# Attention and a gated MLP: the first batch's product with v, split into two 64-column halves of the array

## The chip, the cores and the metric

The kernel runs on one core of a Trainium2 chip. The metric is the device time of one execution in microseconds. Three timed runs of the kernel before gave 475.4, 476.24 and 478.64 us; the median is 476.24 us. One more execution was taken with the hardware profiler, and all rows below are from it. The engines are named as in the profile: PE is TensorE's matmul, PEld its weight load, DVE is VectorE, ACT is ScalarE, POOL is GpSimd, SP is SyncE, which issues the transfers.

## The reference

Attention with a local window of 96 positions and 8 global positions, for 4 batches of 8 heads, 768 positions, 64 numbers per head; behind it a gated MLP that mixes positions.

```python
scores = scale * np.matmul(q, k.transpose(0, 1, 3, 2))
keep = is_global | is_local
scores = np.where(keep, scores + bias, -1000000000.0)
a = np.exp(scores - np.max(scores, axis=-1, keepdims=True))
a = a / (np.sum(a, axis=-1, keepdims=True) + 1e-09)
x = np.matmul(a, v)                    # heads side by side: (4, 768, 512)
h = np.maximum(x @ w_in, 0.0)          # (.., 1024)
u, v = h[..., :512], h[..., 512:]
v_n = (v - mu) / np.sqrt(var + 1e-06)
v_s = np.einsum('ts,bsd->btd', w_spatial, v_n) + b_spatial[None, :, None]
out = (u * v_s) @ w_out
```

## The kernel before

A batch has 6 blocks of 128 positions; a block has 4 pairs of heads. Block n is one of 24. For a block, `prep(n)` loads q and k, `prep_v(n)` loads v, `scores(n)` forms scores and probabilities, and `values(n)` multiplies them with v. Only two 128-wide chunks of keys matter to a block: its own and the one before it, into whose first rows the global positions are copied. The first block of a batch has one chunk. Behind the attention stand the MLP's parts: `mlp_v` (the half that is normalised), `mlp_u` (the other half), `mlp_s` (the mixing of positions) and `mlp_o` (the last product). Their weights are loaded and split into a high and a low half by `setup_w_in`, `setup_w_t` and `setup_w_out` while the first batch's attention runs.

The first batch (`whole(n)`, n under 6) works in full float32; the later batches work with numbers split in two halves of type float32r. In the first batch, for each pair g of heads, `values(n)` does this. The probabilities of both heads are transposed into a PSUM tile `p` (PE), which ACT copies to the SBUF tile `pth`, one of two buffers. Then PE multiplies: the stationary operand is 128 columns of `vring` (64 of each head), the moving operand is all 256 columns of `pth` (128 positions for the first head, 128 for the second), and the result goes to `ops`, 128 partitions by 256 columns. Of this result only half is used: partitions 0 to 63 (first head's v) with columns 0 to 127 (first head's positions), and partitions 64 to 127 with columns 128 to 255. For every second g the sums of the softmax, transposed as well (`raw` to `p`, copied to a tile that is shown as `c`), divide the used parts of two pairs: one DVE instruction for partitions 0 to 63 and one for 64 to 127, each 64 partitions by 256 numbers. The quotient is split into `xth` and `xtl`, the MLP's input.

A float32 matmul stands in the trace as two MATMUL records with a LDWEIGHTS record each; a float32r matmul and a transpose as one.

The order of the work is not that of the code. Every operation is recorded, given a rank from the table `KEYS` (one number for each block and part), and `plan` lays them out on each engine by rank and by its own cost figures. PE and all other engines then carry out their queues in that fixed order. Where the plan has a wait of over 900 ns on PE in the first 150 us, `keep_warm` puts dummy transposes of `ident` there, whose results nobody reads; they run whether or not the wait comes.

All recorded operations have one line in the profile, L39, that of the recorder's `issue`. So tiles are told apart by name: `s` are scores in PSUM, `pr` probabilities, `p` transposes, `pth` their copies, `ops` the product with v, `c` the quotient (and the divisor), `m` all PSUM tiles of the MLP, `raw`, `rawh` and `u` the staging of weights.

Of the kernel before, what the change touches and what calls it, by code (L numbers as in the profile page):

```python
# [10 lines left out]
F32 = mybir.dt.float32  # L11
# [19 lines left out]
class Op:  # L31
# [6 lines left out]
    def issue(self):  # L38
        getattr(self.real, self.call)(*self.args, **self.kw)  # L39

# [17 lines left out]
class Recorder:  # L58
# [26 lines left out]

    def add(self, engine, call, args, kw):
        op = Op()
        op.ways = ((engine, call, args, kw),)
        op.token = self.now
        op.take(0)  # L90
        outs = [kw[x] for x in ("out", "accum_out") if x in kw]
        ins = [x for n, x in kw.items() if n not in ("out", "accum_out") and isinstance(x, bass.AP)]
        aps = [x for x in args if isinstance(x, bass.AP)]
        if "out" not in kw:
            outs.insert(0, aps.pop(0))
        op.writes, op.reads = outs, ins + aps
        op.num = len(self.ops)
        self.ops.append(op)
# [72 lines left out]
def elements(ap):  # L171
    n = 1
    for x in list(ap.ap)[1:]:
        n *= x[1]
    return n
# [19 lines left out]
def cost(op):  # L195

    out = op.writes[0]
    n = elements(out)
    src = op.reads[0] if op.reads else out
    psum = any(in_psum(x) for x in op.reads + op.writes[:1])  # L200
    parts = list(out.ap)[0][1]
    if op.eng == "tensor":
        if op.call == "transpose":
            return 109, 0, False
        n = elements(op.kw["rhs"])
        if op.kw["rhs"].dtype == F32:
            return 4 * max(n, 128) * .422, 0, False
        return {128: 110, 256: 119, 384: 175, 512: 231}[n], 0, False
    if op.eng == "sync":
        return 650, 2050 + n * 4 * parts * .0042, False  # L210
    if op.eng == "scalar":
        if "accum_out" in op.kw:
            return 280 + .83 * n, 90, False
        if in_psum(src):
            return (175 + .85 * n, 0, False) if parts < P else (70 + .86 * n, 0, False)
        return 112 + .83 * n, 0, False
    if op.eng == "gpsimd":
        if n <= 8:
            t = 600 if op.kw.get("op") == ALU.pow else 280
        elif op.call == "tensor_tensor":  # L220
            t = 148 + 2.21 * n
        elif op.kw.get("op0") == ALU.max:
            t = 210 + 3.34 * n
        elif isinstance(op.kw.get("scalar1"), bass.AP):
            t = 270 + .9 * n
        else:
            t = 155 + .84 * n
        return t, 0, True
    one = "accum_out" in op.kw or psum or op.call in ("bn_stats", "bn_aggr", "reciprocal", "tensor_reduce", "memset")
    if op.call == "reciprocal":  # L230
        return 90 + 6.25 * n, 85, False
    pointers = sum(isinstance(op.kw.get(x), bass.AP) for x in ("scalar1", "scalar2"))
    if op.call in ("tensor_scalar", "tensor_copy") and not one:
        return (70 + n if pointers == 2 else 70 + 58 * pointers + .53 * n), 0, True
    if op.call in ("tensor_reduce", "bn_stats"):
        return 120 + 1.06 * elements(src), 0, False
    if op.call == "bn_aggr":
        return 145, 0, False
    return (180 if parts < P else 66) + (1.04 if parts < P else 1.1) * n, 0, not one


def link(ops):

    wrote, used, bank = {}, {}, {}
    for op in ops:
        preds = set()
        for ap in op.reads:
            name, p0, p1, bits = extent(ap)
            for q0, q1, b, o in wrote.get(name, ()):
                if q0 < p1 and p0 < q1 and b & bits:  # L250
                    preds.add(o)
        op.after = set(preds)
        for ap in op.writes:
            name, p0, p1, bits = extent(ap)
            for table in (wrote, used):
                for q0, q1, b, o in table.get(name, ()):
                    if q0 < p1 and p0 < q1 and b & bits:
                        preds.add(o)
        for ap in op.reads:
            name, p0, p1, bits = extent(ap)  # L260
            used.setdefault(name, []).append((p0, p1, bits, op.num))
        for ap in op.writes:
            name, p0, p1, bits = extent(ap)
            for table in (wrote, used):
                if name in table:
                    table[name] = [x for x in table[name] if not (p0 <= x[0] and x[1] <= p1 and x[2] | bits == bits)]
            wrote.setdefault(name, []).append((p0, p1, bits, op.num))
        if op.eng == "tensor":
            name = extent(op.writes[0])
            half = name[0], name[3].bit_length() > 1024  # L270
            if half in bank:
                preds.add(bank[half])
            bank[half] = op.num
        preds.discard(op.num)
        op.preds = preds
# [874 lines left out]
```

## Time and profile before

| | |
|---|---|
| median of three timed runs | 476.24 us |
| the profiled execution's own span | 473.8 us |
| PE busy | 460.7 us (97%) |
| DVE, ACT, POOL busy | 73%, 59%, 54% |
| granted TensorE clock, mean | 0.998 |
| share of PE in the chain that ended last | 87% |
| instructions | 9730 |

The page cuts the span in 40 slices of 11.8 us and gives each engine a digit for its busy tenths. PE's ends are modelled: a stream of matmuls overlaps, so a record is longer than its pace. The pace of a run of n like matmuls is worked out as (length of the run minus one record) divided by (n minus 1). The first batch's attention fills the first 86 us or so of the span, together with the preparation of the weights and the first parts of the MLP.

### The profile page before, as it was taken

Reading aid. Unit: us, or ns where it says so; the run is one execution under the profiler, and the core shown is the slowest. Engines: PE = TensorE matmul, PEld = TensorE weight load, DVE = VectorE, ACT = ScalarE, POOL = GpSimd, SP = SyncE. Lnnn points to the kernel's source line nnn. Section 1 sums busy time; section 2 is a strip of 40 time slices with the busy share of each in tenths; the row PEclk is TensorE's granted clock in tenths of the full one; section 3 lists DMA queues with packets and bytes.
Section 4 is the critical chain, followed back from the end, with each engine's and each line's share of the span. In section 5 each row is a group of like instructions: output and inputs, shape, how many; then the busy total and the mean of one; then the engine's idle time right before and its main releaser. Section 6 shows DMA issues by size and latency. Waiting matters only on the chain.

```text
span 473.8 us, 9730 instructions
## 1 busy us (share of the span) xinstructions
PE 460.7 (97%) x3181; PEld 424.3 (90%) x3181; DVE 344.6 (73%) x1016; ACT 279.9 (59%) x775; POOL 254.1 (54%) x378
## 2 busy tenths in 40 slices
PE   7889999999999999999999999999999999999995
PEld 6668888999999889999999999999989899999994
DVE  6899998948679987986766668784376998843332
ACT  5859896455477776786446448872155888721111
POOL 4334743377575788788545357883037775650000
PEclk9999999999999999999999999999999999999999
DMA  6947323747758687746582167630077683000111
GB/s 212 318 155 229 116 65 114 193 108 183 184 148 226 166 226 193 172 129 166 150 219 101 49 184 187 177 98 19 22 183 209 176 213 78 13 1 1 46 46 50
DMA packets 35915, 65.48 MB, mean 138 GB/s; under 512 B 6064, under 2 KB 6320, under 8 KB 35856
## 3 DMA queue, kind: packets, MB, share of 16 engines
q1 hardware_dynamic: 35856, 64.77, 49.7%
q8 instruction: 27, 0.44, 0.4%
q14 instruction: 32, 0.26, 0.2%
HBM read 29.76 MB, written 6.68 MB: 77 GB/s over the span
## 4 chain that ended last, share of the span: by engine, by line
PE 87%; DVE 4%; SPq 3%; DMA 2%; ACT 2%; issue 1%; DVEq 0%
PE m L39 61%; PE ops L39 9%; PE s L39 9%; PE p L39 8%; SPq L39 3%; DMA vring<-in_v_dram 2%; DVE c L39 1%; ACT pr L39 1%; DVE raw L39 1%; DVE ev L39 0%; DMA kring<-rawh 0%; DVE pr L39 0%; DVE w_in_h L39 0%; DVE rawh L39 0%; DVE xtl L39 0%
## 5 line engine op out<-in xcount | busy, mean ns | idle before, releaser
L39 ACT ACTIVATE pr<-pr,mn 128x256 f32<-128x256 f32 (+1 forms) x192 | 92.0, 483 | 17.5 <-DVE mn L39 17.1
L39 DVE TENSOR_TENSOR c<-ops,c 64x256 f32<-64x256 f32 x168 | 70.6, 421 | 11.0 <-ACT c L39 4.7
L39 DVE CUSTOM_DVE_ANT_0 pr<-s,bias 128x256 f32<-128x256 f32 (+1 forms) x192 | 68.6, 394 | 11.0 <-PE s L39 8.4
L39 POOL TENSOR_SCALAR pr<-pr,rc 128x256 f32<-128x256 f32 (+1 forms) x144 | 68.1, 493 | 10.4 <-DVE rc L39 8.3
L39 PE MATMUL s<-kring,q 128*128 128x256 f32 (+1 forms) x384 | 69.8, 307 | 1.3 <-DVE mn L39 1.0
L39 PE MATMUL ops<-pth,vring 128*128 128x256 f32 x352 | 67.0, 311 | 0.7 <-DVE pth L39 0.5
L39 PEld LDWEIGHTS s<-kring,q 128*128 128x128 f32 x384 | 57.6, 191 | 7.1 <-DVE mn L39 2.4
L39 ACT ACTIVATE pth<-p 128x512 fp32r<-128x512 f32 (+3 forms) x96 | 52.3, 559 | 15.1 <-PE p L39 11.5
L39 PEld LDWEIGHTS ops<-pth,vring 128*128 128x128 f32 x352 | 53.1, 189 | 5.4 <-DVE pth L39 1.2
L39 PE MATMUL p<-ident,pr 128*128 128x128 f32 x352 | 56.6, 273 | 0.7 <-ACT c L39 0.7
L39 DVE TENSOR_TENSOR pth<-p,pth 128x512 fp32r<-128x512 f32 (+1 forms) x72 | 45.1, 642 | 7.0 <-ACT pth L39 6.0
L39 DVE TENSOR_TENSOR ev<-m,b_bc 128x512 f32<-128x512 f32 x24 | 16.6, 691 | 46.1 <-PE m L39 46.0
L39 PEld LDWEIGHTS p<-ident,pr 128*128 128x128 f32 x352 | 42.2, 140 | 5.2 <-ACT c L39 1.3
L39 ACT ACTIVATE ev<-m 128x512 f32<-128x512 f32 (+1 forms) x36 | 21.3, 591 | 42.8 <-PE m L39 40.8
L39 PE MATMUL m<-w_t_h,vnh 128*128 128x256 f32 x288 | 43.9, 282 | 0.0
L39 PE MATMUL m<-w_t_h,vnl 128*128 128x256 f32 x288 | 43.7, 282 | 0.0
L39 PE MATMUL m<-w_t_l,vnh 128*128 128x256 f32 x288 | 43.7, 283 | 0.0
L39 POOL TENSOR_TENSOR xtl<-c,xth 128x256 fp32r<-128x256 f32 x40 | 29.8, 747 | 25.2 <-ACT xth L39 25.1
L39 ACT ACTIVATE gh<-ev 128x512 fp32r<-128x512 f32 x24 | 15.1, 630 | 42.6 <-DVE ev L39 42.6
L39 PEld LDWEIGHTS m<-w_t_h,vnh 128*128 128x128 f32 x288 | 38.9, 189 | 0.7
L39 ACT ACTIVATE c<-ops 64x256 f32<-64x256 f32 x72 | 27.3, 380 | 20.4 <-PE ops L39 17.9
L39 POOL TENSOR_TENSOR vnl<-ev,vnh 128x512 fp32r<-128x512 f32 x24 | 31.1, 1296 | 14.7 <-ACT vnh L39 9.4
(138 smaller groups left out, 997.8 us busy)
## 6 DMA issues: line engine op xcount, KB each, us to landing
q<-rawh SPq DMA_DIRECT2D x72, 128.0 KB, 2.4
q<-raw SPq DMA_DIRECT2D x72, 128.0 KB, 2.4
out_dram<-ev SPq DMA_DIRECT2D x23, 256.0 KB, 2.8
raw<-in_q_dram SPq DMA_DIRECT2D x18, 256.0 KB, 2.9
raw<-in_v_dram SPq DMA_DIRECT2D x18, 256.0 KB, 3.0
raw<-in_k_dram SPq DMA_DIRECT2D x18, 256.0 KB, 3.3
kring<-rawh SPq DMA_DIRECT2D x36, 128.0 KB, 2.4
kring<-raw SPq DMA_DIRECT2D x36, 128.0 KB, 2.4
```

The lines of the kernel that those rows point to most:

```text
L39: getattr(self.real, self.call)(*self.args, **self.kw)
```

## The change

Three things are changed, all else is new text that is switched off (`ROWS = False`: a like change for the scores).

First, the product with v in the first batch. For two pairs of heads at once, when both `pth` are ready, one group of matmuls is issued without anything in between (`together`). Each head has a matmul of its own: 64 columns of `vring` are stationary, the 128 columns of its own positions are moving, and the result goes to partitions 64j to 64j+63 and columns 0 to 127 of `ops`. So there are twice as many matmuls, each with half the stationary columns and half the moving columns, and heads alternate. A group has 8 matmuls (16 MATMUL records); in the first block, which has one chunk, 4 matmuls (8 records). There are 12 groups, two in each of the six blocks.

Second, the division: the used parts now lie in the same columns, so one DVE instruction of 128 partitions by 256 numbers takes the place of two of 64 by 256.

Third, `KEYS` has new numbers in every place, and `plan` charges a group `SWITCH` more than its matmuls. So the order on every engine is a new one.

```diff
 class Op:
     def issue(self):
+        if self.call == "together":
+            for call, args, kw in self.args:
+                getattr(self.real, call)(*args, **kw)
+            return
         getattr(self.real, self.call)(*self.args, **self.kw)
...
+    def together(self, engine, calls):
+
+        self.add(engine, "together", calls, {})
...
 def cost(op):
...
+        if op.call == "together":
+            return SWITCH + sum(2 * elements(kw["rhs"]) * .422 for _, _, kw in op.args), 0, False
...
+SWITCH = 130
+ROWS, COLS = False, True
-KEYS = {'start': -18.36, ('P', 0): -14.95, ('bias', 0): 12.66, ('S', 0, 0): -4.23, ('S', 0, 1): 10.8, ...
+KEYS = {'start': -301.68, ('P', 0): -119.08, ('bias', 0): -61.19, ('S', 0, 0): 120.07, ('S', 0, 1): 67.02, ...
...
 values(n), first batch
                 if g % 2 == 0:
                     ops = opsring[g // 2]
-                for c in range(nch):
+                    pair = []
+                pair.append(pth)
+                if COLS and g % 2:
+                    nc.together(nc.tensor, [
+                        ("matmul", (ops[64 * j:64 * j + 64, x, 0:P],), dict(
+                            lhsT=vring[:, order[c], (g - 1 + x) * P + 64 * j:(g - 1 + x) * P + 64 * j + 64],
+                            rhs=pair[x][:, c, j * P:(j + 1) * P], start=(c == 0), stop=(c == nch - 1),
+                        ))
+                        for x in range(2) for c in range(nch) for j in range(2)
+                    ])
+                for c in range(0 if COLS else nch):
                     nc.tensor.matmul(
                         ops[:, g % 2], lhsT=vring[:, order[c], g * P:(g + 1) * P], rhs=pth[:, c],
...
+                    if COLS and folded(n):
+                        nc.vector.tensor_tensor(out=xs, in0=ops[:, :, 0:P], in1=div, op=ALU.mult)
                     for half, s_ in enumerate(halves):
-                        src = ops[s_, :, half * P:half * P + P]
+                        if COLS and folded(n):
+                            continue
+                        src = ops[s_, :, 0 if COLS else half * P:P if COLS else half * P + P]
```

What it makes of the queues is shown at three places. In these rows a repeat count stands at the end, a float32 matmul counts once, and L39 of before is L41 (a group) or L43 (all else) in the changed kernel.

PE, the third block's product with v and what lies around it, before and then after; `p` are transposes, `s` the next blocks' scores, `ops` the product:

```order
L39 MATMUL ops_93<-pth_125,vring_114 128x256 x2
L39 MATMUL ops_93<-pth_127,vring_114 128x256 x2
L39 MATMUL p_124<-ident,pr_107 128x128 x2
L39 MATMUL p_124<-ident,pr_108 128x128 x2
L39 MATMUL ops_94<-pth_125,vring_114 128x256 x2
L39 MATMUL p_126<-ident,raw_113 128x128 x2
L39 MATMUL p_124<-ident,pr_109 128x128 x2
L39 MATMUL p_124<-ident,pr_110 128x128 x2
L39 MATMUL ops_94<-pth_127,vring_114 128x256 x2
```

```order
L41 MATMUL ops_93<-pth_125,vring_114 64x128 x4
L41 MATMUL ops_93<-pth_127,vring_114 64x128 x4
L43 MATMUL s_106<-kring_97,q_0_96 128x256 x2
L43 MATMUL p_124<-ident,pr_107 128x128 x2
L43 MATMUL p_124<-ident,pr_108 128x128 x2
L43 MATMUL p_126<-ident,raw_113 128x128 x2
L43 MATMUL p_124<-ident,pr_109 128x128 x2
L43 MATMUL p_124<-ident,pr_110 128x128 x2
L41 MATMUL ops_94<-pth_125,vring_114 64x128 x4
L41 MATMUL ops_94<-pth_127,vring_114 64x128 x4
```

The second half of the block's product was in two parts with transposes between them, each behind its own `pth`; now all of it stands behind both.

PE, the first block: what lies between its scores and the second block's, before and then after; `m<-ident` are dummies:

```order
L39 MATMUL m_135<-ident 128x128 x8
L39 MATMUL p_124<-ident,raw_113 128x128 x2
L39 MATMUL p_126<-ident,pr_109 128x128
L39 MATMUL p_126<-ident,pr_110 128x128
L39 MATMUL p_124<-ident,pr_111 128x128
L39 MATMUL p_124<-ident,pr_112 128x128
L39 MATMUL ops_93<-pth_125,vring_114 128x256
L39 MATMUL ops_93<-pth_127,vring_114 128x256
```

```order
L41 MATMUL ops_93<-pth_125,vring_114 64x128 x2
L41 MATMUL ops_93<-pth_127,vring_114 64x128 x2
L43 MATMUL m_135<-ident 128x128 x13
L43 MATMUL p_126<-ident,raw_113 128x128 x2
L43 MATMUL p_124<-ident,raw_113 128x128 x2
L43 MATMUL p_126<-ident,pr_104 128x128 x2
L43 MATMUL p_126<-ident,pr_105 128x128
```

The dummies moved behind the first group and grew from 8 to 13. Over the whole program, after the 17 at the start, there were dummies of 8, 5, 5 and 6; now there are 6, 13, 5, 7 and 7, the last 7 ahead of the sixth block's `mlp_v`.

DVE, the end of the first piece of `w_in` that the MLP needs (`CAST w_in_h`), before and then after; `ISA pr` are the scores with bias and their minimum, `c<-ops` the division, `SCALAR_TENSOR_TENSOR raw` the last steps of unpacking the weight:

```order
L39 TENSOR_TENSOR c_0_128<-ops_94,c_2_134 64x256
L39 TENSOR_SCALAR raw_0_116<-raw_0_116 128x512
L39 TENSOR_TENSOR c_0_128<-ops_94,c_2_134 64x256
L39 SCALAR_TENSOR_TENSOR raw_0_116<-u_115,raw_0_116 128x512
L39 ISA pr_104,mn_101<-s_103,bias 128x256
L39 ISA mn_101 128x1
L39 SCALAR_TENSOR_TENSOR raw_0_116<-u_115,raw_0_116 128x512
L39 TENSOR_TENSOR xtl_123<-c_0_128,xth_122 128x2x128
L39 CAST w_in_h<-raw_0_116 128x512
```

```order
L43 TENSOR_TENSOR xtl_123<-c_1_129,xth_122 128x2x128
L43 SCALAR_TENSOR_TENSOR raw_0_116<-u_115,raw_0_116 128x512
L43 ISA pr_111,mn_101<-s_103,bias 128x256
L43 ISA mn_101 128x1
L43 SCALAR_TENSOR_TENSOR raw_0_116<-u_115,raw_0_116 128x512
L43 TENSOR_TENSOR c_0_128<-ops_94,c_2_134 128x256
L43 CAST w_in_h<-raw_0_116 128x512
```

Ahead of this cast DVE has, of all rows of its queue that differ, two `ISA pr` with their two reads of the minimum, two net divisions, one `CAST xth` and one `xtl` less, and one copy to `c` and one copy to `raw` more. The matmul that waits for this cast is the MLP's first in both orders. On SP the first piece of `w_in` (512 KB) is now issued ahead of the second block's q and k instead of right behind them; transfers in all are the same in number and size.

## Rows read from the trace of the kernel before

**Rows 1.** The page: span, PE, granted clock, and the last chain by engine.

```profile
span 473.8 us, 9730 instructions
PE 460.7 (97%) x3181; PEld 424.3 (90%) x3181; DVE 344.6 (73%) x1016; ACT 279.9 (59%) x775; POOL 254.1 (54%) x378
PEclk9999999999999999999999999999999999999999
PE 87%; DVE 4%; SPq 3%; DMA 2%; ACT 2%; issue 1%; DVEq 0%
```

**Rows 2.** Stretches: length, each engine's busy us (instructions), clock, DMA share, GB/s.

```profile
core 0: us, PE busy (x) PEld busy (x) DVE busy (x) ACT busy (x) POOL busy (x), PEclk, DMA share, GB/s
10.00:20.00 10.00, 8.70 (x44) 6.57 (x43) 8.58 (x36) 9.21 (x35) 4.07 (x4) 1.00 1.04 347
20.00:30.00 10.00, 8.17 (x48) 6.59 (x47) 9.84 (x23) 5.10 (x14) 2.68 (x2) 1.00 0.80 236
...
50.00:60.00 10.00, 10.00 (x58) 8.77 (x57) 9.04 (x28) 8.41 (x21) 6.88 (x8) 1.00 0.36 119
60.00:70.00 10.00, 10.00 (x64) 8.70 (x63) 9.88 (x36) 9.04 (x27) 3.77 (x6) 1.00 0.11 35
```

**Rows 3.** PE in order of time: start, length, instructions [idle before, releaser].

```profile
15.22 1.04 PE L39 MATMUL m<-ident 128*128 128x128 f32 x8
...
17.64 1.13 PE L39 MATMUL ops<-pth,vring 128*128 128x256 f32 x4
...
20.34 1.03 PE L39 MATMUL ops<-pth,vring 128*128 128x256 f32 x4
...
28.56 0.50 PE L39 MATMUL m<-w_in_h,xth 128*128 128x512 f32 x1 [1.83 <-DVE w_in_h L39]
...
39.49 1.89 PE L39 MATMUL ops<-pth,vring 128*128 128x256 f32 x8
```

**Rows 4.** The product with v alone, in two stretches of the first batch.

```profile
0.00:36.00 36.00, 6.37 (x24) 4.16 (x24) 3.35 (x8) 0.00 (x0) 1.00 0.72 229
36.00:86.00 50.00, 16.22 (x64) 11.43 (x64) 5.88 (x14) 0.00 (x0) 1.00 0.42 132
```

**Rows 5.** PE and PEld: later one-pass (float32r) matmuls, 256 and 128 moving columns.

```profile
460.60 0.87 PE L39 MATMUL m<-w_t_h,vnh 128*128 128x256 f32 x6
...
103.81 1.00 PE L39 MATMUL s<-kring,q 128*128 128x128 f32 x8
...
103.69 0.98 PEld L39 LDWEIGHTS s<-kring,q 128*128 128x128 f32 x8
```

**Rows 6.** Groups by form: count, busy us, mean ns of one record, idle before.

```profile
L39 PE MATMUL ops<-pth,vring 128*128 128x256 f32 x64 | 16.2, 383 | 0.0
...
L39 PE MATMUL m<-w_t_h,vnh 128*128 128x256 f32 x6 | 0.9, 281 | 0.0
...
L39 PEld LDWEIGHTS s<-kring,q 128*128 128x128 f32 x8 | 1.0, 191 | 0.0
```

**Rows 7.** DVE in order of time, around the first divisions and the cast.

```profile
20.59 0.24 DVE L39 CAST xth<-c 128x256 fp32r<-128x256 f32 x1
...
21.21 0.42 DVE L39 TENSOR_TENSOR xtl<-c,xth 128x256 fp32r<-128x256 f32 x1
21.55 0.42 DVE L39 CUSTOM_DVE_ANT_0 pr<-s,bias 128x256 f32<-128x256 f32 x1
...
21.89 0.42 DVE L39 COPY raw<-rc 128x512 f32<-128x512 f32 x1
...
22.56 0.41 DVE L39 TENSOR_TENSOR c<-ops,c 64x256 f32<-64x256 f32 x1
22.90 0.41 DVE L39 TENSOR_SCALAR raw<-raw 128x512 int32<-128x512 int32 x1
...
26.48 2.02 DVE L39 CAST w_in_h<-raw 128x512 fp32r<-128x512 f32 x1
```

**Rows 8.** The last chain in its last stretch: start, length, what.

```profile
439.93 25.06 PE m L39 x182
```

More of the change, by code (lines that the diff above doesn't have):

```diff
@@ L38, in issue, with sides @@
     def issue(self):
+        if self.call == "together":
+            for call, args, kw in self.args:
+                getattr(self.real, call)(*args, **kw)
+            return
         getattr(self.real, self.call)(*self.args, **self.kw)
+def sides(call, args, kw):
+    outs = [kw[x] for x in ("out", "accum_out") if x in kw]
+    ins = [x for n, x in kw.items() if n not in ("out", "accum_out") and isinstance(x, bass.AP)]
+    aps = [x for x in args if isinstance(x, bass.AP)]
+    if "out" not in kw:
+        outs.insert(0, aps.pop(0))
+    return outs, ins + aps
 class Engine:
@@ L90, in add @@
         op.take(0)
[L91 to L96, printed above, removed]
+        op.writes, op.reads = [], []
+        for one in args if call == "together" else ((call, args, kw),):
+            outs, ins = sides(*one)
+            op.writes += outs
+            op.reads += ins
         op.num = len(self.ops)
@@ L268, in link @@
         if op.eng == "tensor":
[L269 to L273, printed above, removed]
+            for ap in op.writes:
+                name = extent(ap)
+                half = name[0], name[3].bit_length() > 1024
+                if half in bank:
+                    preds.add(bank[half])
+                bank[half] = op.num
         preds.discard(op.num)
@@ L691, in prep @@
             q1 = ring["q", n % 2]
-            for half in range(2):
+            if ROWS:
+                nc.sync.dma_start(out=q1, in_=q[b, i])
+            for half in range(0 if ROWS else 2):
                 s_ = slice(64 * half, 64 * half + 64)
@@ L762, in scores @@
                 yield
-            sp = ps_s.tile([P, 2, W], F32, name="sp", tag="s")
-            for j in range(2):
+            tiled = ROWS and whole(n)
+            if tiled and g % 2 == 0:
+                rows = [ps_s.tile([P, 2, W], F32, name="sp", tag="s") for _ in range(2)]
+                nc.together(nc.tensor, [
+                    ("matmul", (rows[j][:, x],), dict(lhsT=q1[64 * j:64 * j + 64, g + x], rhs=kring[64 * j:64 * j + 64, sl, g + x], start=True, stop=True))
+                    for x in range(2) for j in range(2)
+                ])
+            sp = None if tiled else ps_s.tile([P, 2, W], F32, name="sp", tag="s")
+            for j in range(0 if tiled else 2):
                 h = 2 * g + j
@@ L776, in scores @@
                 nc.vector.tensor_tensor_reduce(
-                    out=pr, in0=sp[:, j], in1=bt, scale=-scale, scalar=3e38, op0=ALU.add, op1=ALU.min,
+                    out=pr, in0=rows[j][:, g % 2] if tiled else sp[:, j], in1=bt, scale=-scale, scalar=3e38, op0=ALU.add, op1=ALU.min,
                     accum_out=mn[:, h:h + 1],
```

7 lines of the change are left out of this document (6 added, 1 removed).

## The prediction

> **What bounds the kernel now.** I read the page first, then busy time by stretch, then PE in order of time. On the page PE is busy 97% of the span, at full granted clock throughout, and the last chain lies on PE for 87% [rows 1]. So time is won or lost on PE, in the stretches where PE has no spare time. From 50 us on PE is busy 10.00 of 10 us, while from 10 to 30 us it is busy only 8.70 and 8.17 of 10 [rows 2]. There it waits: the largest wait, 1.83 us, is for the first piece of `w_in` from DVE, at 28.56 us [rows 3]. DVE is busy 9.84 of 10 us just then [rows 2]. So there are two regimes: a start, until about 36 us, paced by DVE and the transfers, and the rest, paced by PE.
>
> The product with v in the first batch has 88 records, 24 before 36 us and 64 between 36 and 86 us [rows 4]. Eight of them in a stream take 1.89 us, one record is 0.383 us long [rows 3, 6], so the pace is (1.89 - 0.383) / 7 = 0.215 us. The whole is 88 x 0.215 = 18.9 us of PE: 5.2 us at the start and 13.8 us in the stretch that PE paces. That second figure is what the change can work on.
>
> **What the matmuls cost afterwards.** 64 records become 128, each with half the moving columns. By columns one such record is 0.215 / 2 = 0.108 us. If a head's record runs in its half of the array while the other head's runs in the other half, two share that time, 0.054 us each, and 128 take 6.9 us: 6.9 us saved. If they run one after the other, 128 x 0.108 = 13.8 us and nothing is saved. No row of before has two matmuls side by side, so these are the two ends. A row that warns stands further on: one-pass matmuls with 256 columns follow each other every (0.87 - 0.281) / 5 = 0.118 us, but with 128 columns their weight loads, and so they, still need (0.98 - 0.191) / 7 = 0.113 us [rows 5, 6]. Halving the columns bought nothing there; the load of 128 weight columns sets the pace. The change halves the stationary columns too. If a load shrinks with its columns it is 0.056 us and just keeps up with 0.054; if not, 0.113 us a record undoes the gain. I take the first: half the weights move in a load, and heads alternate, so that a load can go to the half that is free.
>
> The Trainium skill, "TensorE: Matmul & The Clock Gate", section "Step-by-step: what each phase is for", says that a load's time goes by its column count. By that rule the load is the 0.056 us of the sum, and no run here shows it yet.
>
> **What a group costs at its ends.** Eight groups lie in the stretch that PE paces (two in each of blocks 2 to 5), so 16 ends. The trace has no change between whole and half array. Bounds from the nearest rows: nothing; or a weight load that nothing covers, as for the first product at 17.64 us, 1.13 us for four against 1.03 us for the next four, 0.10 us [rows 3]; or that and the emptying of the last matmul as well, record less pace, 0.383 - 0.215 = 0.17 us [rows 6], 0.27 us together. I take 0.10 us, the one wait that a row shows on PE by itself: 16 x 0.10 = 1.6 us (0 to 4.3).
>
> The Trainium skill, "TensorEngine Tiling (Array Packing)", section "Key Properties", says that a change of tiling mode drains TensorE. By that rule the price is the full 0.27 us, and the sum of this term 4.3 us; that is the second rival below, and the trace so far neither shows nor excludes it.
>
> **Dummies.** Eight dummies in a stream take 1.04 us, about 0.11 us each once the last one's tail is taken off [rows 3]. Where the start now has 24 (6, 13, 5) it had 18; they fill waits there, and if the waits come they cost nothing, else 6 x 0.11 = 0.7 us. Behind it there were 6 and now are 14: 8 x 0.11 = 0.9 us of PE. I charge that in full, since PE has no waits there.
>
> **The division.** A half division's record is 0.41 us and the next instruction starts 0.34 us after it; 128 partitions with as many numbers from PSUM, the scores with bias, take 0.42 us and 0.34 us [rows 7]. So twelve divisions by 0.34 us fall away, 4.1 us of DVE. From 36 us on PE covers this and it is worth nothing by itself. At the start DVE sets the pace. Ahead of the cast that the first MLP matmul waits for, DVE loses two minima (2 x 0.34), two divisions (2 x 0.34), an `xth` cast and an `xtl` (0.24 + 0.42) and gains two copies (2 x 0.34): 1.3 us less [rows 7]. Against it, on SP 512 KB of `w_in` now go ahead of the second block's q and k: at 347 GB/s and a DMA share of 1.04 [rows 2] these land 1.5 us later. DVE has weight steps to do meanwhile, so I take half of what it saves: the MLP starts 0.7 us earlier (from 1.5 us later to 1.5 us earlier). The PE time saved before the cast buys nothing: PE only waits longer at 28.56 us.
>
> **Late in turn.** A group needs both `pth`, and holds both until its end, where before the first pair's product ran ahead and gave its buffer back. Queued behind a waiting group on PE are the next blocks' scores and MLP matmuls, and for the scores DVE and ACT wait. In the MLP stretch the order puts other matmuls between; in the first two blocks there are none yet, which is where the 13 dummies stand. I count it in the bounds of the start. The end of the program is untouched: the last 25 us of the chain on PE are the last batch's mixing and last product [rows 8], in the same order as before.
>
> **Sum.** -6.9 (product) + 1.6 (ends) + 0.9 (dummies) - 0.7 (start) = -5.1 us. The profiled span of 473.8 us becomes 468.7. The median of the runs is 2.4 us above that span; I let that stand: 476.24 - 5.1 = 471.1 us. A measurement here tells a difference from none at about 1%, 4.8 us, so the forecast lies close to the border at 471.5.
>
> **Rivals.**
> 1. Forecast, chance 0.49: 471.1, with its own range 468.5 to 473.5 (ends at 0 to 0.2 us, start at 0 to 1.5 us).
> 2. Every end costs a drain and an uncovered load, 0.27 us: 16 x 0.17 = 2.7 us more, 473.8. For: loads go ahead of matmuls all over the trace, and this could stop at an end. Against: between transposes and matmuls, the other change of kind on PE, the rows show no idle time ahead of a product [rows 3]. Chance 0.14.
> 3. PE is faster, but what feeds it is not: DVE and ACT are busy 9.88 and 9.04 of 10 us from 60 to 70 us [rows 2], and the last 7 dummies stand ahead of the sixth block's `mlp_v`, a place without dummies before. Then up to 86 us the gain is DVE's: eight late divisions by 0.34 us, 2.7 us, less the 0.9 us of dummies, 474.4. Against: DVE is at 9.04 from 50 to 60 us, and PE at 10.00 the whole time. Chance 0.14.
> 4. The other side: loads do not shrink, or halves do not overlap. Pieces at 0.113 us: 128 x 0.113 = 14.5 us, 0.7 us more than before; ends 1.6 to 4.3; dummies 0.9; the start none or 1 us, since its groups lengthen as well. 3.2 to 6.9 us slower, 479.4 to 483.1. It decides above the pace at which pieces, ends and dummies add up to 13.8 us: (13.8 - 1.6 - 0.9) / 128 = 0.088 us. For: the 0.113 us of the row above. Against: those loads have 128 columns. Chance 0.11.
> 5. The new order takes most of the start's waits away, 1.83 us and more, and the ends cost nothing: -6.9 + 0.9 - 2.5 = -8.5, 467.7. Chance 0.12.
>
> **How the numbers follow.** Range 467.5 to 478.0: it takes in cases 1 to 3, the greater part of case 5 and none of case 4's upper part; about 0.18 is left out. Faster by over 1% (under 471.5): case 5 and seven tenths of case 1, 0.12 + 0.34 = 0.46. Slower by over 1% (over 481.0): six tenths of case 4, and 0.03 for a start that slips and brings case 2 or 3 with it: 0.10. The rest, 0.44, is within 1%.
>
> **What would show it.** In the profile after, a group of 16 records should take about 0.9 us plus a tail (1.72 us before for the eight of a group): near 1.8 us it is case 4. The start of the next matmul behind a group, less the last record's pace, gives an end's price. PE busy from 40 to 90 us below 9.9 of 10, with DVE or ACT as releaser, is case 3. The first `m<-w_in_h` should start near 27.9 us. Behind 90 us every piece of work should run about 5 us earlier with nothing new on PE. The forecast is wrong if the whole product is not shortened, if PE waits in the first batch, or if the new order costs PE waits in the later batches, for which I have counted nothing in either direction.

## The result, and the profile after

The changed kernel takes 479.37 us (477.32 to 482.89, 18 runs) where the kernel before, run beside it, takes 475.59 us (474.54 to 478.64, 18 runs). The ratio is 1.0071 with a 95% interval of 1.0054 to 1.0087: 0.7% slower, 3.4 us (the two medians by themselves lie 3.8 us apart). The forecast was 471.1 us, and the range ended at 478.0. The granted clock makes little of it: its mean over the 18 runs is 0.997, and 0.998 over 18 runs of the kernel before that were taken with the first experiments; the difference is worth under 1 us, an estimate.

The product did get shorter, as the next rows show, and PE waits longer. The execution that was profiled is, with 477.33 us (475.3 of it the span), one of the two shortest of the 18, so it shows less loss than the median has.

The page of the kernel after, for [rows 1]:

```profile
span 475.3 us, 9930 instructions
PE 459.1 (97%) x3283; PEld 418.8 (88%) x3283; DVE 344.6 (72%) x1011; ACT 274.2 (58%) x767; POOL 255.9 (54%) x379
PEclk9999999999999999999999999999999999999999
PE 80%; DVE 7%; ACT 4%; DMA 3%; POOL 2%; issue 2%; SPq 1%; ACTq 0%; POOLq 0%; DVEq 0%
```

The chain that ended last lies on PE for 80% and no longer for 87%; DVE, ACT and POOL have come into it. The stretches of the kernel after, for [rows 2] (length; busy us and instructions of PE, weight load, DVE, ACT, POOL; clock, DMA share, GB/s):

```profile
10.00:20.00 10.00, 8.03 (x48) 6.02 (x49) 7.95 (x34) 9.22 (x37) 3.26 (x3) 1.00 1.04 367
20.00:30.00 10.00, 9.98 (x84) 7.61 (x83) 10.00 (x34) 7.50 (x22) 1.68 (x3) 1.00 0.70 224
30.00:40.00 10.00, 7.57 (x53) 6.25 (x52) 9.97 (x26) 6.89 (x20) 5.66 (x5) 1.00 0.68 211
40.00:50.00 10.00, 8.64 (x58) 6.83 (x57) 9.12 (x32) 8.84 (x26) 5.09 (x5) 1.00 0.72 213
50.00:60.00 10.00, 9.64 (x74) 7.82 (x73) 9.18 (x29) 8.15 (x28) 5.89 (x7) 1.00 0.22 70
60.00:70.00 10.00, 9.41 (x77) 6.69 (x75) 9.14 (x28) 9.15 (x25) 6.40 (x9) 1.00 0.14 42
```

PE is now full from 20 to 30 us, where it waited before. But from 30 to 70 us, where from 36 us on the forecast held it to be the bound, it stands idle for 2.43 + 1.36 + 0.36 + 0.59 = 4.7 us. The product alone in two stretches, for [rows 4]:

```profile
0.00:36.00 36.00, 3.50 (x48) 2.54 (x48) 1.68 (x4) 0.00 (x0) 1.00 0.79 260
36.00:86.00 50.00, 8.76 (x128) 6.82 (x128) 3.34 (x8) 0.00 (x0) 1.00 0.41 121
```

In the second stretch it keeps PE busy for 8.76 us and not 16.22. PE in order of time in the kernel after, for [rows 3]:

```profile
23.34 0.60 PE L43 MATMUL p<-ident,pr 128*128 128x128 f32 x4
23.87 1.09 PE L41 MATMUL ops<-pth,vring 128*64 128x128 f32 x16
24.90 0.44 PE L43 MATMUL p<-ident,raw 128*128 128x128 f32 x2
25.09 0.48 PE L43 MATMUL m<-w_in_h,xth 128*128 128x512 f32 x1
...
36.84 1.13 PE L43 MATMUL s<-kring,q 128*128 128x256 f32 x4 [2.43 <-DVE mn L43]
...
41.46 0.66 PE L43 MATMUL p<-ident,pr 128*128 128x128 f32 x4 [0.53 <-ACT pth L43]
...
44.47 0.44 PE L43 MATMUL p<-ident,pr 128*128 128x128 f32 x2 [0.75 <-ACT pth L43]
```

A group of sixteen pieces starts at 23.87 us and what follows it at 24.90 us. The first MLP matmul comes at 25.09 us with no wait; before, it came at 28.56 us after a wait of 1.83 us. The largest wait has moved to 36.84 us: scores of a later block wait 2.43 us for DVE's minima. What DVE and POOL did then (DVE in order of time, with POOL's instructions among them):

```profile
31.01 1.83 POOL L43 TENSOR_TENSOR w_t_l<-vring,w_t_h 128x768 fp32r<-128x768 f32 x1
...
31.15 0.41 DVE L43 CUSTOM_DVE_ANT_0 pr<-s,bias 128x256 f32<-128x256 f32 x1
...
31.49 1.63 DVE L43 TENSOR_TENSOR xtl<-c,xth 128x256 fp32r<-128x256 f32 x1
...
32.81 1.00 POOL L43 TENSOR_SCALAR w_t_h<-vring 128x768 fp32r<-128x768 f32 x1
...
33.04 1.05 DVE L43 TENSOR_SCALAR rawh<-rawh 128x512 f32<-128x512 f32 x1
...
33.90 1.85 POOL L43 TENSOR_TENSOR w_t_l<-vring,w_t_h 128x768 fp32r<-128x768 f32 x1
...
34.13 1.91 DVE L43 TENSOR_SCALAR rawh<-rawh 128x512 int32<-128x512 int32 x1
```

Three DVE instructions that take 0.41 to 0.42 us elsewhere take 1.63, 1.05 and 1.91 us, and each ends 0.28 or 0.29 us after a POOL instruction: 33.12 after 32.84, 34.09 after 33.81, 36.04 after 35.75. It looks as if each waits until POOL's instruction is through and only then does its work (a hold-off, in what follows). The Trainium skill, "SBUF — State Buffer", section "Who interferes with whom", says just that of these two engines: DVE's two-port modes, and its instructions with two inputs in SBUF, need a pair of ports that it shares with GpSimd (POOL here), and whichever comes first holds it for its whole instruction. These rows agree. So do the minima of the scores between them, whose scores lie in PSUM: `pr<-s,bias` at 31.15 us takes its usual 0.41 us beside the first of these POOL instructions.

### The profile page after: what moved, and what is told of

Same layout as the page of the kernel before. It is cut to its first block, busy times and chain, and to the rows that moved or that the text cites. A ratio compares the mean times of both kernels' runs of the same rounds, so it can differ in the third digit from the quotient of the medians.

```text
span 475.3 us, 9930 instructions
## 1 busy us (share of the span) xinstructions
PE 459.1 (97%) x3283; PEld 418.8 (88%) x3283; DVE 344.6 (72%) x1011; ACT 274.2 (58%) x767; POOL 255.9 (54%) x379
## 4 chain that ended last, share of the span: by engine, by line
PE 80%; DVE 7%; ACT 4%; DMA 3%; POOL 2%; issue 2%; SPq 1%; ACTq 0%; POOLq 0%; DVEq 0%
PE m L43 58%; PE s L43 8%; PE p L43 6%; PE ops L43 6%; PE ops L41 2%; DVE raw L43 1%; SPq L43 1%; DMA u<-in_moe_w_in_dram 1%; DVE pr L43 1%; ACT pth L43 1%; DVE c L43 1%; DVE rawh L43 1%; DMA q<-raw 1%; DVE ev L43 1%; ACT pr L43 1%
## 5 line engine op out<-in xcount | busy, mean ns | idle before, releaser
L43 ACT ACTIVATE pr<-pr,mn 128x256 f32<-128x256 f32 (+1 forms) x192 | 91.7, 480 | 10.8 <-DVE mn L43 10.5
L43 DVE CUSTOM_DVE_ANT_0 pr<-s,bias 128x256 f32<-128x256 f32 (+1 forms) x192 | 68.0, 394 | 11.8 <-PE s L43 9.2
L43 POOL TENSOR_SCALAR pr<-pr,rc 128x256 f32<-128x256 f32 (+1 forms) x144 | 69.6, 503 | 11.2 <-DVE rc L43 9.2
L43 PE MATMUL s<-kring,q 128*128 128x256 f32 (+1 forms) x384 | 71.1, 309 | 4.2 <-DVE mn L43 3.3
L43 DVE TENSOR_TENSOR c<-ops,c 64x256 f32<-64x256 f32 (+1 forms) x156 | 65.5, 420 | 8.6 <-ACT c L43 5.1
L43 ACT ACTIVATE pth<-p 128x512 fp32r<-128x512 f32 (+3 forms) x96 | 51.5, 558 | 29.3 <-PE ops L43 15.6
L43 PEld LDWEIGHTS s<-kring,q 128*128 128x128 f32 x384 | 57.1, 191 | 9.9 <-DVE mn L43 5.1
L43 PE MATMUL p<-ident,pr 128*128 128x128 f32 x352 | 57.9, 275 | 3.2 <-ACT pth L43 1.9
L43 PEld LDWEIGHTS p<-ident,pr 128*128 128x128 f32 x352 | 41.8, 140 | 9.9 <-ACT pth L43 3.1
L43 DVE TENSOR_TENSOR ev<-m,b_bc 128x512 f32<-128x512 f32 x24 | 16.6, 691 | 45.6 <-PE m L43 45.6
L43 DVE TENSOR_TENSOR pth<-p,pth 128x512 fp32r<-128x512 f32 (+1 forms) x72 | 45.1, 641 | 5.8 <-ACT pth L43 4.7
L43 PE MATMUL ops<-pth,vring 128*128 128x256 f32 x264 | 45.2, 288 | 0.0
L43 PE MATMUL m<-w_t_h,vnh 128*128 128x256 f32 x288 | 44.4, 283 | 0.0
L43 PE MATMUL m<-w_t_h,vnl 128*128 128x256 f32 x288 | 44.1, 283 | 0.0
L43 PE MATMUL m<-w_t_l,vnh 128*128 128x256 f32 x288 | 43.8, 282 | 0.0
L43 ACT ACTIVATE gh<-ev 128x512 fp32r<-128x512 f32 x24 | 15.1, 630 | 48.6 <-DVE ev L43 48.5
L43 POOL TENSOR_TENSOR xtl<-c,xth 128x256 fp32r<-128x256 f32 x40 | 30.7, 769 | 21.6 <-ACT xth L43 21.3
L43 ACT ACTIVATE ev<-m 128x512 f32<-128x512 f32 (+1 forms) x36 | 21.2, 588 | 34.0 <-PE m L43 33.6
L43 PEld LDWEIGHTS m<-w_t_h,vnh 128*128 128x128 f32 x288 | 39.0, 189 | 0.8
L43 PEld LDWEIGHTS ops<-pth,vring 128*128 128x128 f32 x264 | 37.7, 189 | 2.1 <-ACT pr L43 0.4
L43 PEld LDWEIGHTS m<-w_t_l,vnh 128*128 128x128 f32 x288 | 38.3, 189 | 0.3
L43 PEld LDWEIGHTS m<-w_t_h,vnl 128*128 128x128 f32 x288 | 38.3, 189 | 0.0
```

## Experiments: the order and the product apart

The change has three parts: the product in halves, one division for both heads, and a new plan, that is, a new order of everything. In these runs "before's order" means every engine's instructions in the order of the kernel before, row by row, with only the rows of the product and its division exchanged; likewise for "the new order".

**Before's order, the product in halves.** The plan is made on the old matmul, and two pieces are issued in its place:

```diff
 for c in range(nch):
-    nc.tensor.matmul(ops[:, g % 2], lhsT=vring[:, order[c], g * P:(g + 1) * P], rhs=pth[:, c], ...)
+    for j in range(2):   # issued at the place of the one above
+        nc.tensor.matmul(ops[64*j:64*j+64, g % 2, 0:P], lhsT=vring[:, order[c], g*P+64*j:g*P+64*j+64], rhs=pth[:, c, j*P:(j+1)*P], ...)
```

> The kernel before, with its order on every engine kept row by row; each 256-column product with v is issued as two 64-column matmuls of 128 moving columns in its place, and the two half divisions stay. Theory A (the halves save PE time and the new order lost it): the 32 products of blocks 2 to 5 save 0.43 - 0.21 us each less ends, about 4 us, so about 471.5 us, ratio 0.991. Theory B (the first batch is paced by DVE, ACT and transfers, so PE time saved in it comes back as waits whatever the order): within 1 us of before, ratio 0.998 to 1.002, with PE's waits up by about what the product saved. Ends take more here than in the change, as there are more of them.

Measured: 474.76 us, ratio 0.9974 (0.9962 to 0.9987).

**The same with one division** of 128 partitions, the second half division dropped:

> As the kernel with the order kept, and one division of 128 partitions in the place of the first of two halves; the second is left out of DVE's queue. Theory A: 471 us or a little less. Theory B: DVE gets 12 x 0.34 = 4.1 us back in the stretch it paces, so 1 to 3 us faster than with two halves.

Measured: 473.88 us, ratio 0.9952 (0.9933 to 0.9971); the interval overlaps the one above, so the division's own share isn't shown. This beats both kernels, with the new instructions in the old order. In this order the pieces stand in 19 runs and not in the 12 groups of the change. With 0.054 us a piece and 0.26 us for going in and out of a run (both worked out below), PE's work on the product falls by 18.9 - 176 x 0.054 - 19 x 0.26 = 4.5 us, an estimate; the time falls by 2.3.

**The two sets of ranks exchanged.** `KEYS` of before in the changed kernel, and `KEYS` of the change with `COLS = False`, planned anew in both:

> The changed kernel with the ranks of before, all else as changed: groups, one division, the planner's charge for a group. The order is then planned anew from the old ranks. Theory A: faster than before, 470 to 473 us, since only the ranks are put back. Theory B: 474 to 477 us, since both ranks meet the same start.

> The changed kernel with the product and the division as before, and the new ranks. Theory A: the new ranks alone lose what the product saves and 3.4 us more: about 483 us, ratio 1.015. Theory B: the new ranks are no worse by themselves, 475 to 478 us.

Measured: 520.7 us, ratio 1.0942, and 494.47 us, ratio 1.0393. With other costs than those that a set of ranks was found with, the plan is worse in the later batches too, where the product wasn't changed (PE is busy 109.29 and 116.93 of 120 us from 120 to 240 us, 119.36 before). So this pair says nothing on what the order in the changed kernel costs, and the next run replaced it.

**The new order, the whole product.** Each group of sixteen pieces issues four matmuls of 128x256, and the division its two halves:

```diff
-sixteen ("matmul", (ops[64*j:64*j+64, x, 0:P],), dict(lhsT=..64 columns.., rhs=pair[x][:, c, j*P:(j+1)*P]))
+four    ("matmul", (ops[:, x],), dict(lhsT=vring[:, order[c], (g-1+x)*P:(g+x)*P], rhs=pair[x][:, c]))
```

> The changed kernel's order on every engine, row by row, but each head pair's product with v again as the kernel before has it: four matmuls of 128x256 in place of sixteen 64-column pieces, and the division in its two halves. Beside the runs with before's order this fills the square of two orders by two products. Theory A (the halves save about 6 us of TensorE time in any order; the new order itself costs it back): 479.4 + 6 = about 485 us, and PE waits as long as in the changed kernel. Theory B (the first batch is paced by what feeds PE, so that TensorE time taken from the product comes back as waits in any order): 479 to 481 us, with PE's waits between 30 and 90 us shorter by what the product grew.

Measured: 486.1 us, ratio 1.0228 (1.0201 to 1.0255). Theory A stands in this order: the halves and the one division are worth 1.0228 - 1.0071 = 1.57%, 7.5 us. And the new order by itself costs 2.28%, 10.8 us, with the whole product, and 1.0071 - 0.9952 = 1.19%, 5.7 us, with the halves. So the new order costs more than the halves bring in before's order.

**Less product.** Only the first of two key chunks, in either order: 80 of 176 pieces fewer, 4.3 us of TensorE time.

```diff
-start=(c == 0), stop=(c == nch - 1) for c in range(nch)
+start=True, stop=True               for c = 0 alone
```

> The changed kernel with only the first of the two key chunks of each product with v in the first batch: 80 of the 176 pieces are left out, 80 x 0.054 = 4.3 us of TensorE time, and nothing else moves. Where TensorE paces the first batch in the new order: 479.4 - 4.3 = about 475 us. Theory B, something else paces it: 478.5 to 479.4 us, and PE's waits grow by nearly 4 us.

> The same piece left out (80 of 176 pieces, 4.3 us of TensorE time) of the kernel that has before's order, the product in halves and one division (473.9 us). Where TensorE still paces the first batch in that order: about 469.6 us. Theory B: 473 to 474 us, and PE's waits grow by what was taken out.

Measured: 477.18 us, ratio 1.0042 (1.0022 to 1.0062), in the new order; 471.54 us, 0.9921 (0.9895 to 0.9947), in before's. Taking out 4.3 us of TensorE time brings 1.4 and 1.5 us, a third; with these intervals each gain may lie anywhere between nothing and 3 us. Most of what is taken out beyond the halves comes back: in before's order PE's idle time between 5 and 100 us grows from 95 - 90.15 = 4.9 to 95 - 87.92 = 7.1 us. PE's waits up to 100 us in the changed kernel and in this one without half the product (total us, times, longest):

```profile
PE s L43 <- DVE mn L43: 3.3, 3, 2.4
PE p L43 <- ACT pth L43: 1.9, 4, 0.7
```

```profile
PE s L41 <- DVE mn L41: 7.0, 5, 2.5
PE p L41 <- ACT pth L41: 2.0, 4, 0.8
```

The waits for DVE's minima grow from 3.3 to 7.0 us, but not all of that is the product's: the second execution is a long one (480.07 us), and 1.9 us of the growth is a wait at 15.76 us (2.47 us for 0.56), ahead of the first piece that was left out.

## Experiments: what the new order collides with

**Three of the twelve operations on w_t left out**, those of POOL at 31 to 36 us of the rows above:

```diff
+ w_t_h of tile 2, w_t_l of tiles 1 and 2: filled by ACT before 6 us, not computed by POOL
```

> The changed kernel with three of the twelve operations that split w_t left out, the ones that POOL runs between 31 and 36 us (w_t_l of tiles 1 and 2, w_t_h of tile 2); ACT fills these places with a constant before 6 us, where it is idle, so that part of w_t is not the input's. If the wait of 2.43 us of PE at 36.84 us comes from DVE running slowly beside POOL (1.05 and 1.91 us for two operations that take 0.43 and 0.42 elsewhere): these two are back near 0.42, the wait is under 0.5 us, and the time is up to 2 us shorter, 477.4 us. If the slow DVE operations have another cause: they stay at 1 to 2 us, and so does the wait. If the wait goes and the time stays within 0.5 us of 479.4, the later waits give it back, as theory B has it.

Measured: 475.36 us, ratio 1.0008 (0.9988 to 1.0028), 0.63% or 3.0 us below the changed kernel. The two slow DVE instructions are back at 0.42 us:

```profile
34.49 0.42 DVE L41 TENSOR_SCALAR rawh<-rawh 128x512 f32<-128x512 f32 x1
...
35.35 0.42 DVE L41 TENSOR_SCALAR rawh<-rawh 128x512 int32<-128x512 int32 x1
```

The wait near 36.8 us is gone. In the execution that was profiled another one of the kind stands earlier, beside the operations on tile 0, that were left in:

```profile
15.77 3.55 PE L41 MATMUL s<-kring,q 128*128 128x256 f32 x8 [2.38 <-DVE mn L41]
```

```profile
14.00:16.00 2.00, 0.23 (x1) 0.23 (x2) 2.00 (x8) 0.93 (x2) 0.49 (x1) 0.89 1.08 284
16.00:18.00 2.00, 2.00 (x5) 1.62 (x6) 1.20 (x7) 1.93 (x9) 0.00 (x0) 0.50 0.99 370
```

Here the granted clock also fell to 0.50 after PE had been busy 0.23 of 2 us, and eight score matmuls took 3.55 us where the profile of the changed kernel has 1.99 us for them, after a wait of 0.56 us. The changed kernel with half the product, which has the changed kernel's instructions and no others up to this place, waits 2.47 us here too. So the same program has a long wait at such a place in one execution and a short one in another, and one profile can miss it.

**The same work in shorter POOL operations.** This needs nothing left out:

```diff
 hi_lo(st, w_t_h[:, t], w_t_l[:, t], E("wth", t), E("wtl", t))
+# where POOL has them: w_t_h issued in 2 operations of 384 columns, w_t_l in 4 of 192, in place of one of 768
```

> The changed kernel, with POOL's splitting of w_t issued in pieces: each w_t_l in four operations of 192 columns in place of one of 768 (1.82 us), each w_t_h of POOL's in two; the same work, order and engines. If DVE is held off for as long as one operation of POOL lasts, a DVE operation that meets one loses about 0.5 us and not 1.5 to 2. The run without three of these operations was 0.63% (3.0 us) below the changed kernel; pieces should bring half to two thirds of that: 476.7 to 477.2 us where the changed kernel stands at 478.7 (1.0071 times its neighbour before). If DVE and POOL merely slow each other in proportion to their work: no change, 478.7 us or slightly more for the overhead of the added POOL operations.

> The same pieces in the kernel with before's order, the product in halves and one division (0.9952 of before, 473.1 us). There DVE lost 1.6 us to one w_t_l at 26.5 us, ACT waited 2.9 us for it and PE 2.2 us. With pieces: that wait of PE under 1.2 us, and 472 to 472.5 us, a ratio of 0.993 to 0.9945. Without an effect of the length of POOL's operations: 0.995 again.

> The same pieces in the kernel before, as a control: its PE waited 1.83 us for w_in_h at 28.56 us, which DVE cast in 2.02 us beside POOL. If that is the same hold-off, and PE paces what follows: 1 us less, a ratio near 0.998. If the kernel before is paced elsewhere in its first batch: 1.000.

Measured: 474.58 us, ratio 0.9969 (0.9952 to 0.9986), in the changed kernel; 472.05 us, 0.9917 (0.9891 to 0.9942), with before's order, halves and one division; 475.46 us, 0.9988 (0.9971 to 1.0005), in the kernel before. DVE and POOL at the same place in the changed kernel with pieces:

```profile
31.44 2.82 POOL L44 TENSOR_TENSOR w_t_l<-vring,w_t_h 128x192 fp32r<-128x192 f32 x4
...
31.92 0.41 DVE L50 TENSOR_TENSOR xtl<-c,xth 128x256 fp32r<-128x256 f32 x1
32.26 0.81 DVE L50 TENSOR_SCALAR rawh<-rawh 128x512 f32<-128x512 f32 x1
...
33.13 0.67 DVE L50 TENSOR_SCALAR rawh<-rawh 128x512 int32<-128x512 int32 x1
```

The three DVE instructions take 0.41, 0.81 and 0.67 us, 1.9 us together and not 4.6, though POOL itself needs longer (2.82 us for a w_t_l of 1.83). The scores no longer wait, and PE is busy from 30 to 40 us for 9.47 us and not 7.57:

```profile
30.00:40.00 10.00, 9.47 (x69) 7.79 (x70) 9.96 (x30) 9.38 (x27) 9.12 (x13) 1.00 0.61 179
```

The changed kernel gains 1.02%, 4.9 us, more than the 1.5 to 2 expected. The order of every engine's instructions is the same in both, so what POOL's long operations cost in this order is more than the whole loss of the change. Before's order with halves gains 0.35%, 1.7 us, with intervals that overlap. The kernel before gains 0.12%, which isn't told from nothing: the wait of 1.83 us for `w_in_h` is gone from its profile, but one of 1.3 us for a `pth` has come in. Before's order with halves and pieces is the fastest so far, 0.8% under the kernel before.

## Experiments: what is left of the new order's cost

Between the new order with pieces (0.9969) and before's with pieces (0.9917) half a per cent is left, 2.5 us (0.5%, give or take 0.3).

**More places for pth**, to test the wait for both `pth` of a group. First in the free second halves of the two slots:

> The changed kernel with four places for pth in place of two in the first three blocks of the first batch (the free second halves of the same two slots), so that ACT needn't wait for a group of sixteen pieces to give both places back; order as in the changed kernel. If the group's wait for both pth costs time: PE's waits for pth at 41.46 and 44.47 us (0.53 and 0.75 us) and ACT's wait at 42.81 us (0.64 us) go, and the time is about 1 us below the changed kernel, 477.7 us where that stands at 478.7. If these waits only fill time that the next wait would take: 478.7 us.

Measured: 483.85 us, ratio 1.0158. The second halves aren't free: `w_out` is staged there from 12.99 us on, so that this kernel writes over a part of it, and ACT's copy waits 5.97 us for that transfer at 22.80 us, and PE 4.25 us for the copy. Nothing follows from it on the question. Then in two places that are empty in the first three blocks, on top of the pieces:

```diff
+more_pth = [work.tile([P, 2, 2 * P], F32, tag=x) for x in ("gh", "gl")]   # second pair of heads, blocks 0 to 2
```

> The changed kernel with w_t in pieces (474.6 us, 0.9969 of before) and with four places for pth in the first three blocks, the two added ones in places that hold nothing until later in the batch (gh, gl). Order unchanged. If a group's wait for both pth makes up what the new order still costs: PE's waits for pth at 39.23 and 42.25 us (0.53 and 0.75 us) go and the ratio falls by 0.2 to 0.3%, to about 0.994 to 0.995. If those waits only fill time that the next wait would take: 0.997.

Measured: 473.48 us, ratio 0.9953 (0.9935 to 0.997), an interval that overlaps the 0.9969 without. PE in order of time:

```profile
38.35 0.66 PE L48 MATMUL p<-ident,pr 128*128 128x128 f32 x4 [0.53 <-ACT gl L48]
...
41.37 0.44 PE L48 MATMUL p<-ident,pr 128*128 128x128 f32 x2 [0.75 <-ACT pth L48]
```

The two waits of 0.53 and 0.75 us stand as before. So they aren't for the place of `pth`; by the rows' releasers a transposition waits until ACT has copied out one of the PSUM tiles `p`. That a group holds both `pth` isn't shown to cost anything: the two ratios differ by 0.16%, less than their intervals.

**The whole product in the new order, with pieces:**

> The new order with the whole product (four matmuls of 128x256 for sixteen pieces, two half divisions: 1.0228 of before) and with w_t in pieces. It fills the second square: two orders by two products, both without the long POOL operations. If the hold-off of DVE is most of what the new order cost: about 1.0228 - 0.0102 = 1.0126 or less, and the halves then bring 1.0126 - 0.9969 = 1.6% in this order. If the new order costs by itself when its groups take longer: 1.018 to 1.023.

Measured: 482.18 us, ratio 1.0125 (1.0101 to 1.015): the pieces bring 1.03% here too, and the halves again 1.0125 - 0.9969 = 1.56%. The two gains add up. But with the whole product the new order still costs 1.0125 - 0.9988 = 1.37%, 6.5 us, without the long POOL operations, where it cost 2.28% with them: they are part of what the new order costs, not all of it.

**Fewer dummies**, by `WARM_TO = 45000`:

> The changed kernel with w_t in pieces, less the two groups of seven dummies at 61.62 and 89.34 us (0.98 and 0.93 us busy). If they lie on PE's path: 1.6 to 1.9 us less, 472.8 us, a ratio of about 0.9935. If they lie in waits, or hold the clock up: 474.6 us (0.997), or more where the granted clock falls after a wait there.

Measured: 474.42 us, ratio 0.9973 (0.9954 to 0.9991), against 0.9969: no difference, and by the intervals no saving above about 1 us, where 1.6 to 1.9 would have come if the dummies lay on PE's path. Where they stood, PE waits:

```profile
61.72 0.44 PE L50 MATMUL p<-ident,raw 128*128 128x128 f32 x2 [0.80 <-ACT pth L50]
...
89.42 1.19 PE L50 MATMUL m<-w_in_h,gh 128*128 128x512 f32 x4 [0.69 <-ACT u L50]
```

**Less product in before's order with pieces:**

> The kernel with before's order, halves, one division and pieces (472.05 us, 0.9917) with 80 of the 176 pieces of the product left out, 4.3 us of TensorE time (only the first of two key chunks is multiplied). With the long POOL operations the same cut brought 1.5 us (0.9952 to 0.9921). If DVE's hold-off was what ate the rest: 3 to 4 us here, a ratio of 0.983 to 0.985. If the first batch is paced by DVE and ACT in any case: 1 to 1.5 us, 0.989.

Measured: 472.67 us, ratio 0.9922 (0.9894 to 0.9951), against 0.9917. Without the hold-off, cutting another 4.3 us from the product brings nothing that shows (by the intervals at most 1.6 us): PE waits for ACT, DVE and POOL, one after the other, and in the profiled execution, the longest of the six, the clock falls to 0.50 after the wait at 39.40 us:

```profile
39.40 0.66 PE L48 MATMUL p<-ident,pr 128*128 128x128 f32 x4 [1.47 <-ACT c L48]
```

```profile
42.00:44.00 2.00, 2.00 (x9) 1.60 (x8) 2.00 (x5) 1.38 (x4) 0.73 (x1) 0.50 0.37 93
```

All ratios to the kernel before, side by side:

| product | POOL's w_t | before's order | new order |
|---|---|---|---|
| whole | long | 1 | 1.0228 |
| whole | pieces | 0.9988 | 1.0125 |
| halves, one division | long | 0.9952 | 1.0071 (the change) |
| halves, one division | pieces | 0.9917 | 0.9969 |
| half of it, in halves | long | 0.9921 | 1.0042 |
| half of it, in halves | pieces | 0.9922 | not run |

## Why the prediction was wrong

**The pieces: right.** Sixteen of them take 1.09 us, and less a record's 0.273 us that is (1.09 - 0.273) / 15 = 0.054 us a piece, as forecast. So loads do shrink with their columns and halves do overlap; rival 4 names a time close to the measured one, 479.4 us, but its mechanism isn't there. In one and the same order the halves and the one division are worth 7.5 us, more than the forecast's whole gain.

**A group's ends: right within a little.** Four transpositions at 23.34 us have the group behind them after 0.53 us where they need 4 x 0.11 = 0.44; the group needs 24.90 - 23.87 = 1.03 us and not 16 x 0.054 = 0.86. That is 0.09 us going in and 0.17 coming out, 0.26 us a group, 0.13 an end, where 0.10 was taken. Eight groups cost 2.1 us, so PE's work on the product falls from 13.8 to 8 x (0.86 + 0.26) = 9.0 us in the later stretch, by 4.8 us, where 6.9 - 1.6 = 5.3 were forecast. The full drain of 0.27 us an end, the second rival, isn't there.

**The start: sign right, too small, and in part luck.** The first MLP matmul comes at 25.09 us, 3.5 us earlier, where 0.7 was taken. Of that, 1.6 us is the cast of `w_in_h` itself, which took 2.02 us beside a long POOL operation and takes 0.42 us in the new order; the prediction didn't have that. The wait for `w_in` is gone, as rival 5 has it, and a longer one stands 12 us later.

**The dummies: wrong.** 0.9 us was charged for eight; dropping fourteen changes nothing that shows, and PE waits where they stood.

**The step that failed** is the border at 36 us, behind which "the rest" is "paced by PE", and with it the sum, which but for the dummies has no term for what the new order does behind that border. From 5.1 us faster to 3.4 us slower are 8.5 us: the new instructions bring 2.3 us and not 5.1 in before's order, 2.8 us; POOL's long operations cost the new order 3.2 us more than the old one; 2.5 us stay open. Two things are wrong in the step.

First, no row that the prediction names shows the border. [rows 2] has PE full from 50 us on. The stretches between, in the kernel before, are these:

```profile
30.00:40.00 10.00, 9.83 (x56) 8.10 (x55) 9.53 (x36) 8.55 (x27) 4.99 (x6) 1.00 0.55 183
40.00:50.00 10.00, 9.55 (x54) 7.94 (x53) 9.86 (x29) 8.43 (x25) 4.62 (x4) 1.00 0.53 172
```

PE isn't full there and DVE nearly is. Of the 4.7 us that PE stands idle between 30 and 70 us in the changed kernel, 2.43 + 1.36 = 3.8 lie in these 20 us. And a PE that is busy 10.00 of 10 us shows that this order, at this length of the product, is fed; it doesn't show how much shorter the product may get. In before's order the halves and one division bring 2.3 us of the 4.5, and with short POOL operations 0.9988 - 0.9917 = 0.71%, 3.4 us, so most of it; another 4.3 us taken out brings 1.5 us or nothing. By the prediction's own sign, PE below 9.9 of 10 us between 40 and 90 us with ACT as releaser, rival 3 is what came in the changed kernel. But rival 3 still had a gain of 1.8 us, and the largest wait, at 36.84 us, stands ahead of that stretch and is for DVE.

Second, the new order was costed only by what it moves: steps, queues, buffers. It also moves which POOL operation meets which DVE instruction. Of the 5.7 us that the new order costs with halves, (1.0071 - 0.9969) - (0.9952 - 0.9917) = 0.67%, 3.2 us (0.67%, give or take 0.4), go when POOL's operations on w_t are cut into pieces; with the whole product it is 1.03 - 0.12 = 0.91%. The evidence was in [rows 7], a cast of `w_in_h` at 26.48 us of 2.02 us. It ends at 28.50 us, 0.28 us after this POOL instruction of the kernel before:

```profile
26.37 1.85 POOL L39 TENSOR_TENSOR w_t_l<-vring,w_t_h 128x768 fp32r<-128x768 f32 x1
```

I took the wait behind it, 1.83 us, as DVE's being busy, and didn't ask why a cast should take five times what its neighbours take. With that seen, a rival on the slower side, DVE held off at a place on which the scores hang, would have had a price of about 2.02 - 0.42 = 1.6 us a meeting.

**What stays open.** The other half per cent, 2.5 us, of the new order. It is more than it looks, since the new order has 12 runs of pieces for 19 and should by that be 7 x 0.26 = 1.8 us ahead. It isn't the dummies as far as is shown, and not a group's hold on both `pth`. In the profiles of the two kernels with pieces, whose spans are 474.4 and 469.3 us, PE waits 3.8 and 2.8 us between 5 and 100 us, and the new order has 55 dummies for 41, which stand where it would wait, 14 x 0.11 = 1.5 us. Behind 100 us, up to 400, PE is idle for 2.7 and 1.1 us: the new order also waits in the later batches, for which the prediction had counted nothing. That makes 4.1 us where 5.1 + 1.8 = 6.9 are to be explained, and which feeder is behind it isn't settled: up to 100 us, in the new order most of the waiting is for ACT's copies of `pth` out of the PSUM tiles `p` (1.9 us), in before's for its `c` (1.3 us).

## To carry to other kernels

A stretch in which TensorE is busy all the time says little on how much TensorE time can be taken out: ask of each engine that feeds it whether it could go faster, take out more in a trial before planning on the gain, and read every stretch that the gain is to come from. When a change comes with a new order, try the new instructions in the old order, and the new order with the old instructions; here that alone told a gain of 0.5% to 1.6% from a loss of 1.2% to 2.3%. Where a DVE instruction takes several times what the same form takes elsewhere, look whether it ends just behind a POOL instruction, as here. If something hangs on it, try POOL's operation in shorter ones: that brought 1.0% in the new order and nothing that shows in the kernel before.

## What the runs showed of the hardware

DVE instructions of 0.41 to 0.42 us take 1.05 to 2.03 us beside POOL operations on SBUF of 1.0 to 2.1 us (the changed kernel, and before's order with halves and one division), and end 0.28 us after them; with POOL's operations of 0.7 us on the mean (the changed kernel with pieces) they take up to 0.81 us. Four POOL operations of 192 columns take 2.82 us where one of 768 takes 1.83.

A matmul with 64 stationary and 128 moving columns of float32, alternating between the halves of the array, is issued every 0.054 us, so that the two that replace one 128x256 matmul of 0.215 us take half its time; going in and out of a group of them costs 0.26 us together (the same for the groups of 8: what follows the one at 16.81 us comes at 17.40 us, 0.16 us more than 8 x 0.054).

The granted clock: after a wait of PE of 2.19 us that ended at 30.04 us, in before's order with halves and one division, it fell to the lower of the two levels (0.50) for about 3.4 us, which by estimate costs half of that; after the wait of 2.43 us in the profile of the changed kernel it stayed at 1.00. The rows of the former, in stretches of 1 us:

```profile
31.00:32.00 1.00, 1.00 (x5) 0.85 (x4) 0.77 (x2) 0.61 (x4) 0.00 (x0) 0.63 0.33 25
32.00:33.00 1.00, 1.00 (x5) 0.75 (x4) 0.27 (x1) 0.00 (x0) 0.22 (x1) 0.50 0.79 303
33.00:34.00 1.00, 1.00 (x6) 0.91 (x5) 0.51 (x4) 1.00 (x2) 1.00 (x3) 0.50 0.45 133
34.00:35.00 1.00, 1.00 (x5) 0.86 (x4) 0.85 (x1) 1.00 (x4) 0.92 (x2) 0.67 0.72 219
```
